# Sliding-window attention: score matmuls in two strips of 64 keys by 320 queries in place of four strips of 32 keys by 288 queries

## The chip, the cores and the metric

The kernel runs on one core of one Trainium2 chip, as a single program. The metric is the device time of one execution in microseconds (us); lower is better. The kernel before took 1099.22 us, the median of three runs (1099.03 to 1101.2). One execution was recorded by the profiler; its rows are quoted below. Engines are named as the profile names them: PE does matmuls, PEld is the load of a matmul's stationary operand (its weights), DVE is the vector engine, ACT the scalar engine, POOL is GpSimd, and SP issues the DMAs.

## What is computed

The reference is one transformer block on 2048 tokens of width 640. Only the attention half is touched by the change:

```python
H = 32; Dh = D // H; W = 256                       # D = 640, so Dh = 20
q, k, v = split(layernorm(x) @ wqkv)               # 32 heads
scores = einsum("bhqd,bhkd->bhqk", q, k) * Dh ** -0.5
mask = (i - j >= 0) & (i - j < W)                  # query i, key j
p = softmax(where(mask, scores, -1e9))
h = x + (p @ v).reshape(B, S, D) @ wo
```

A gated MLP with a spatial 2048 x 2048 projection follows (`h2 = h + B(layernorm(h))`). It comes after the attention in time and is not edited.

## The kernel before, in words

**Stages.** The program first forms V, then Q and K (the lines of `qk_item`, L612 to L614), then runs the attention in one long loop over steps `s`, then the output projection (L118) and the gated MLP. The profile shows the attention loop between 237 and 456 us of the span.

**Units and items.** The 32 heads are taken in 8 groups of 4; the 2048 tokens in 16 blocks of 128. A unit `u` is one group and one block, so there are `NU = 128` units, and each has four items, one for each head `hh`. Queries and keys of a group lie in SBUF tiles (`slot` or `xb`) as rows of bf16 parts: 120 rows for the exact product in three bf16 pieces, and three more rows that carry the row maximum of the softmax.

**The loop.** Step `s` does three things on PE, which are interleaved in an order written by hand (PE, DVE, ACT and SP follow the written order here; POOL's order is set by the planner after step 13):

- `max_item` for unit `s + 18` (L373 matmuls, then a DVE maximum, L383): 128 queries against up to 384 keys, to find each query's largest score. It is written as four strips of 32 queries by 288 keys, each on its own quarter of the array's columns: `tile_position=(0, 32 * j)`. It stops at step 109, when no unit is left.
- `score_item` for unit `s` (L426 matmuls, then the exponential on ACT, L429 or, from step 113, L431 for two heads together): 128 keys against up to 384 queries, with the maximum subtracted by the three extra rows. Only 257 of the 384 queries see a given key, so it too is written as strips, four of 32 keys by 288 queries. After the fourth head, POOL sets what lies outside the window to zero (L433, L436).
- `pv_item` for unit `s - 2` (L454 matmuls, f32): four heads at once, on four tiles of 32 columns, accumulated over the key blocks in a PSUM bank. It is issued in two halves, after heads 1 and 3. Finished banks are copied by ACT (L473) or DVE (L475) and stored.

So with heads 0 to 3 the PE order within a step is max, score, max, score, pv, max, score, max, score, pv. From step 110 the max items are gone. In `max_rows` (L389, once in 8 steps) PE turns the row maxima; DVE, POOL and two DMAs then bring them into the three extra rows, 8 or more steps before they are used.

**Buffers.** The maxima have three PSUM banks, the scores three others; the score of an item waits until the exponential of three items ago has freed its bank. In the last steps three pairs of banks serve two heads each.

**Where a strip crosses token 1024.** The tokens of a group lie in two halves, so `tokens` (L346) splits a strip that crosses the middle into two matmuls.

Of the kernel before, what the change touches and what calls it, by code (L numbers as in the profile page):

```python
# [15 lines left out]
P = 128  # L16
# [18 lines left out]
def block_kernel(ctx, tc, x, xt, wqk, wv, wo, w_in, wsp, bsp, w_out, out):  # L35
    nc = tc.nc
# [225 lines left out]
    with ExitStack() as ab:  # L262
# [54 lines left out]
        def s2_tile():  # L317
            return s_tile(2)
# [27 lines left out]
        def tokens(st, rows, a, hh, t0, n):  # L346

            o = 0
            while o < n:
                c, t = divmod(t0 + o, S // 2)  # L350
                w = min(n - o, S // 2 - t)
                yield o, w, st[c][:rows, a, hh, t:t + w]
                o += w

        def one(st, rows, a, hh, t0, n):
            (_, _, x), = tokens(st, rows, a, hh, t0, n)
            return x
# [47 lines left out]
        def score_item(u, hh):  # L405


            g, kb = divmod(u, NT)
            st = slot_ap[g % 3]
            n = min(384, S - kb * P)  # L410
            if hh == 0:
                p_tiles[u] = tmp3.tile([P, 4, 384], F32, tag="pt", bufs=4, name=f"pt{u}")
            pt = p_tiles[u]
            if u > NU - NT:
                if hh % 2 == 0:
                    bank2.append(bank2.pop(0))
                ps = bank2[-1][:, hh % 2]
            else:
                ps = s2_tile()
            for i in range(4):  # L420
                k0 = kb * P + 32 * i
                b, e = 32 * i, min(n, 32 * i + 288)
                if NU - NT < u and 4 * (u - NU + NT - 1) + hh < 6:
                    b, e = 0, n
                for o, w, q in tokens(st, 123, 0, hh, kb * P + b, e - b):
                    nc.tensor.matmul(ps[32 * i:32 * i + 32, b + o:b + o + w], one(st, 123, 1, hh, k0, 32), q,  # L426
                                     start=True, stop=True, tile_position=(0, 32 * i))
            if u <= NU - NT:
                nc.scalar.activation(pt[:, hh, :n], ps[:, :n], AF.Exp, scale=SCALE)  # L429
            elif hh % 2:  # L430
                nc.scalar.activation(pt[:, hh - 1:hh + 1, :n], bank2[-1][:, :, :n], AF.Exp, scale=SCALE)  # L431
            if hh == 3:
                nc.gpsimd.affine_select(out=pt[:, :, :P], in_=pt[:, :, :P], pattern=[[0, 4], [1, P]], base=0,  # L433
                                        channel_multiplier=-1, compare_op=OP.is_ge, fill=0.0)
                if n == 384:
                    nc.gpsimd.affine_select(out=pt[:, :, 256:], in_=pt[:, :, 256:], pattern=[[0, 4], [-1, P]],  # L436
                                            base=-1, channel_multiplier=1, compare_op=OP.is_ge, fill=0.0)
# [41 lines left out]
        if True:  # L479
# [191 lines left out]
            for n in range(7):  # L671
                w = slice(n % 3 * P, (n % 3 + 1) * P)
# [64 lines left out]
            for n in range(24):  # L737
                q, r = divmod(n, 8)
# [49 lines left out]
        for s in range(NU + 2):  # L788
# [9 lines left out]
            for hh in range(4):  # L798
                if s < 2 and hh == 2:
                    next(dense)  # L800
                if s == 1 and hh == 3:
                    assert next(dense, 0) == 0
                if u1 < NU:
                    max_item(u1 // NT, u1 % NT, hh)
                if s < NU:
                    score_item(s, hh)
                if hh == 1 and u1 % 8 == 0 and s <= NU - LEAD:
                    rows = max_rows((u1 - 8) // NT, (u1 - 8) % NT // 8)
                    next(rows)
                if hh == 3 and u1 % 8 == 1 and s <= NU - LEAD + 1:  # L810
                    next(rows)
                if 2 <= s < NU - 1:
                    if hh == 1:
                        pv = pv_item(s - 2)
                        next(pv, None)
                    if hh == 3:
                        next(pv, None)
                for u in {(NU, 1): [NU - 3], (NU + 1, 0): [NU - 2, NU - 1]}.get((s, hh), []):
                    for _ in pv_item(u):
                        pass  # L820
                if (s, hh) in ((NU, 0), (NU + 1, 3)):
                    if s == NU:
                        psB.close()
                        psW = pool(psB, "psW", space=PSUM)
                    pre_ps.append(proj_o(s - NU, psW.tile([P, 2, 512], F32, tag="wo", bufs=3, name=f"wo_ps{s - NU}")))
# [779 lines left out]
```

## Time and profile before

| | |
|---|---|
| median of three runs | 1099.22 us |
| the profiled execution's own time | 1096.99 us |
| its span | 1095.3 us |
| PE busy | 1073.5 us, 98% |
| ACT busy in the attention loop, 236.9 to 431 us | 179.06 of 194.10 us |
| DVE busy there | 182.65 us |
| PE busy there | 188.11 us |
| score matmuls (L426), mean of one | 273 ns (x1296, the largest group) |
| granted PE clock | 1.00 throughout |

The profile gives each matmul a start and a duration. The durations of neighbouring matmuls overlap, since the array is a pipeline: a matmul with 288 columns is shown as 0.29 us, while the next group starts 0.12 us later. So it is the distance from one start to the next that tells what an operation costs on PE, and a group in a timeline row such as "0.31 ... x4" is four matmuls on four column tiles that start almost together. In a row, `123*32 123x288` means weights of 123 rows by 32 columns, and 288 columns streamed past them.

### The profile page before, as it was taken

The numbers are of one execution on the slowest core, as the hardware profiler recorded it, in microseconds if no ns is written. First come the engines' busy times: TensorE is split into PE (matmuls) and PEld (weight loads), VectorE is DVE, ScalarE is ACT, GpSimd is POOL, SyncE is SP. The second block draws the span as 40 slices with busy tenths as digits, with TensorE's granted clock in tenths as the row PEclk, the third lists the DMA queues.
The fourth block names the chain that finished last, engine by engine and source line by source line (L and its number), as shares of the span: only waits on it lengthen the run. The fifth ranks groups of instructions, "written<-read, shape, count | busy, mean of one in ns | idle before, by whom it ended". The sixth has DMA issues, their size and how long they took to land.

```text
span 1095.3 us, 28703 instructions
## 1 busy us (share of the span) xinstructions
PE 1073.5 (98%) x11045; PEld 967.9 (88%) x11045; DVE 779.6 (71%) x2157; ACT 603.7 (55%) x1257; POOL 308.9 (28%) x446
## 2 busy tenths in 40 slices
PE   8999999999999999999999999999999999999998
PEld 8998886668888787699999998999999899999998
DVE  6643445779999997586677678656556899988674
ACT  4444433249989899766766557433358433333331
POOL 4414445668766677622200012000001000000000
PEclk9999999999999999999999999999999999999999
DMA  7834566465665565679845342242341567684542
GB/s 257 296 117 118 174 212 217 150 214 174 191 186 184 187 192 172 193 217 289 316 179 186 113 135 77 71 142 87 126 150 51 176 230 249 231 280 139 181 156 97
DMA packets 92293, 194.78 MB, mean 178 GB/s; under 512 B 11958, under 2 KB 46278, under 8 KB 88262
## 3 DMA queue, kind: packets, MB, share of 16 engines
q1 hardware_dynamic: 92156, 192.95, 54.0%
q8 instruction: 87, 1.43, 0.5%
q14 instruction: 50, 0.41, 0.1%
HBM read 127.90 MB, written 64.95 MB: 176 GB/s over the span
## 4 chain that ended last, share of the span: by engine, by line
PE 84%; DMA 4%; issue 4%; ACT 3%; DVE 2%; POOL 1%; SPq 1%; ACTq 0%; POOLq 0%; DVEq 0%
PE g L1217 23%; PE zb L1102 8%; PE pv L454 7%; PE bank L373 5%; PE bank L426 5%; PE qk L612 4%; PE qk L613 4%; PE qk L614 4%; PE out_x L1381 3%; PE zx L1042 2%; PE out_v L1381 2%; PE zv L1042 2%; PE zy L1042 1%; PE zw L1042 1%; PE bank L377 1%
## 5 line engine op out<-in xcount | busy, mean ns | idle before, releaser
L429 ACT ACTIVATE pt<-bank 128x384 f32<-128x384 f32 (+1 forms) x452 | 180.5, 486 | 14.5 <-PE bank L426 9.7
L1217 PE MATMUL g<-zl,aw 128*128 128x432 f32 x768 | 168.9, 357 | 1.0 <-ACT zl L864 1.0
L383 DVE CUSTOM_DVE_ANT_0 junk<-bank,strip 128x288 bf16<-128x288 f32 x392 | 155.8, 452 | 9.8 <-PE bank L373 5.6
L864 ACT ACTIVATE aw<-fx 128x512 fp32r<-128x512 f32 (+2 forms) x152 | 86.1, 587 | 128.4 <-DVE fx L858 53.6
L1217 PEld LDWEIGHTS g<-zl,aw 128*128 128x128 f32 x768 | 144.0, 188 | 7.4 <-ACT zl L864 1.4
L858 DVE TENSOR_TENSOR aw<-fx,aw 128x512 fp32r<-128x512 f32 (+2 forms) x152 | 95.7, 638 | 58.8 <-ACT aw L864 53.8
L454 PE MATMUL pv<-pt,v_sb 128*32 128x192 f32 (+3 forms) x1984 | 133.3, 322 | 2.9 <-POOL pt L433 1.2
L1217 PE MATMUL g<-ze,aw 128*128 128x432 f32 x576 | 132.6, 359 | 2.3 <-DVE row L858 2.3
L1217 PEld LDWEIGHTS g<-ze,aw 128*128 128x128 f32 x576 | 107.1, 188 | 9.0 <-DVE row L858 3.7
L433 POOL TENSOR_SCALAR_AFFINE_SELECT pt<-pt 128x512 f32<-128x512 f32 x128 | 82.6, 646 | 58.1 <-ACT pt L429 55.1
L426 PE MATMUL bank<-slot 123*32 123x288 bf16 (+8 forms) x1296 | 94.8, 273 | 1.0 <-ACT pt L429 0.6
L373 PE MATMUL bank<-slot 120*32 120x288 bf16 (+4 forms) x1248 | 91.6, 275 | 3.0 <-issue 2.8
L454 PEld LDWEIGHTS pv<-pt,v_sb 128*32 128x32 f32 x1984 | 64.1, 110 | 10.2 <-POOL pt L433 5.1
L436 POOL TENSOR_SCALAR_AFFINE_SELECT pt<-pt 128x512 f32<-128x512 f32 x112 | 71.0, 634 | 0.0
L426 PEld LDWEIGHTS <-slot 123*32 123x32 bf16 x1728 | 59.3, 96 | 11.5 <-issue 1.7
L858 DVE TENSOR_TENSOR row<-g,row 128x432 f32<-128x432 f32 x80 | 48.3, 603 | 21.3 <-PE g L1217 20.9
L373 PEld LDWEIGHTS <-slot 120*32 120x32 bf16 x1408 | 51.0, 95 | 14.0 <-issue 5.6
L383 DVE CUSTOM_DVE_ANT_0 junk<-bank,mask 128x384 bf16<-128x384 f32 (+2 forms) x120 | 51.4, 444 | 16.6 <-PE bank L377 14.7
L645 POOL TENSOR_TENSOR sg<-rest,sg 128x512 bf16<-128x512 f32 x39 | 45.6, 1169 | 57.7 <-ACT sg L644 45.2
L630 DVE TENSOR_TENSOR rest<-qk,std 128x512 f32<-128x512 f32 x36 | 24.8, 690 | 42.4 <-PE qk L614 41.2
L635 ACT ACTIVATE sg<-rest 128x512 bf16<-128x512 f32 x39 | 24.6, 631 | 54.1 <-DVE rest L630 52.3
L118 PE MATMUL wo_ps<-xb,xb 128*128 128x320 f32 x260 | 52.4, 311 | 0.5 <-DVE mvc L1496 0.5
(289 smaller groups left out, 2534.5 us busy)
## 6 DMA issues: line engine op xcount, KB each, us to landing
slot<-qk_d SPq DMA_DIRECT2D x144, 160.0 KB
fx<-wsp_in SPq DMA_DIRECT2D x32, 512.0 KB
qk_d<-sg SPq DMA_DIRECT2D x39, 384.0 KB
o_d<-ot SPq DMA_DIRECT2D x64, 128.0 KB
xb<-qk_d SPq DMA_DIRECT2D x48, 160.0 KB
fx<-hn_d SPq DMA_DIRECT2D x24, 320.0 KB
z_d<-row SPq DMA_DIRECT2D x16, 432.0 KB
g_d<-row SPq DMA_DIRECT2D x16, 432.0 KB
```

The source lines that it names most:

```text
L373: nc.tensor.matmul(ps[32 * j:32 * j + 32, o:o + w], one(st, 120, 0, hh, q0, 32), k, start=True, stop=True, tile_position=(0, 32 * j))
L383: nc.vector.tensor_tensor_reduce(out=junk[:, :n], in0=ps[:, :n], in1=keep, scale=1.0, scalar=NEG, op0=OP.add, op1=OP.max, accum_out=m_cols ...
L426: nc.tensor.matmul(ps[32 * i:32 * i + 32, b + o:b + o + w], one(st, 123, 1, hh, k0, 32), q, start=True, stop=True, tile_position=(0, 32 * i))
L429: nc.scalar.activation(pt[:, hh, :n], ps[:, :n], AF.Exp, scale=SCALE)
L433: nc.gpsimd.affine_select(out=pt[:, :, :P], in_=pt[:, :, :P], pattern=[[0, 4], [1, P]], base=0, channel_multiplier=-1, compare_op=OP.is_ge ...
L436: nc.gpsimd.affine_select(out=pt[:, :, 256:], in_=pt[:, :, 256:], pattern=[[0, 4], [-1, P]], base=-1, channel_multiplier=1, compare_op=OP. ...
L454: nc.tensor.matmul(ps[32 * hh:32 * hh + 32, a - 512 * c:b - 512 * c], v_sb[:, kb, v0:v0 + 32], pt[:, hh, a - kb * P:b - kb * P], start=fir ...
L858: (eng or nc.vector).tensor_tensor(out=out, in0=a, in1=b, op=op)
L864: nc.scalar.activation(out, a, AF.Copy)
L1042: nc.tensor.matmul(ps, a[x], b[:, y], start=start and m + x + y == 0, stop=stop and m == n - 1 and x == 1, skip_group_check=True)
L1102: nc.tensor.matmul(b[0][:, :HF], a[:, x, kk], win2[0][:, y, kk, h * HF:(h + 1) * HF], start=kk + x + y == 0, stop=kk == KD - 1 and x == 1)
L1217: nc.tensor.matmul(ps, w[m][:, x, k], zc[k][m][:, y], start=start and k + x + y == 0, stop=stop and k == 3 and x == 1, skip_group_check=True)
```

## The change

The score item is made of two strips of 64 keys by 320 queries, each on half of the array's columns, in place of four strips of 32 keys by 288 queries. 320 queries are what the window of 64 consecutive keys needs, rounded up to a multiple of 64. The max items and the pv items keep their tiles of 32 columns. The diff is whole:

```diff
@@ -417,14 +417,14 @@ def score_item(u, hh)
-            for i in range(4):
-                k0 = kb * P + 32 * i
-                b, e = 32 * i, min(n, 32 * i + 288)
+            for i in range(2):
+                k0 = kb * P + 64 * i
+                b, e = 64 * i, min(n, 64 * i + 320)
                 if NU - NT < u and 4 * (u - NU + NT - 1) + hh < 6:
                     b, e = 0, n
                 for o, w, q in tokens(st, 123, 0, hh, kb * P + b, e - b):
-                    nc.tensor.matmul(ps[32 * i:32 * i + 32, b + o:b + o + w], one(st, 123, 1, hh, k0, 32), q,
-                                     start=True, stop=True, tile_position=(0, 32 * i))
+                    nc.tensor.matmul(ps[64 * i:64 * i + 64, b + o:b + o + w], one(st, 123, 1, hh, k0, 64), q,
+                                     start=True, stop=True, tile_position=(0, 64 * i))
```

What it does to PE's order in the middle of the loop is seen at the end of an item. Before, one score item and the pv half behind it stand so (LDWEIGHTS is a weight load; `x4` behind an L454 row stands for the four heads):

```order
L426 LDWEIGHTS slot_0_2008
L426 MATMUL bank_131<-slot_0_2008 32x288
L426 LDWEIGHTS slot_0_2008
L426 MATMUL bank_131<-slot_0_2008 32x288
L426 LDWEIGHTS slot_0_2008
L426 MATMUL bank_131<-slot_0_2008 32x288
L426 LDWEIGHTS slot_0_2008
L426 MATMUL bank_131<-slot_0_2008 32x288
L454 MATMUL pv_1_3639<-pt_3538,v_sb 32x256 x4
L373 LDWEIGHTS xb_98
```

Now a score item stands between the last strips of a max item and the pv half:

```order
L373 MATMUL bank_127<-slot_1_2009 32x288
L373 LDWEIGHTS slot_1_2009
L373 MATMUL bank_127<-slot_1_2009 32x288
L426 LDWEIGHTS slot_1_103
L426 MATMUL bank_132<-slot_1_103 64x320
L426 LDWEIGHTS slot_1_103
L426 MATMUL bank_132<-slot_1_103 64x320
L454 MATMUL pv_3_5647<-pt_5562,v_sb 32x256 x4
L373 LDWEIGHTS xb_97
```

Eight rows have become four, and the first number of their last column has gone from 32 to 64: a score item is now the only work in the loop with 64 columns, and 32-column work stands on either side of it. Over the program PE's list falls from 11238 rows to 8934. In the changed order a change from a 32-column row to a 64-column row comes 440 times up to the last max item, and as often back; of the 440 ways back 228 lead to L373, 196 to L454, 14 to L389 and 2 to L612.

In the last steps, where no max items are left, two score items (two heads) now stand together between pv halves:

```order
L454 MATMUL pv_2_8608<-pt_8613,v_sb 32x192 x4
L426 LDWEIGHTS slot_1_2009
L426 MATMUL pair_8375<-slot_1_2009 64x320
L426 LDWEIGHTS slot_1_2009
L426 MATMUL pair_8375<-slot_1_2009 64x320
L426 LDWEIGHTS slot_1_2009
L426 MATMUL pair_8375<-slot_1_2009 64x320
L426 LDWEIGHTS slot_1_2009
L426 MATMUL pair_8375<-slot_1_2009 64x320
L454 MATMUL pv_2_8608<-pt_8648,v_sb 32x256 x4
```

Eight rows stand here where there were sixteen, and the change between 32 and 64 columns comes 34 times each way, once in two items.

On DVE, ACT and SP nothing moves. On POOL the planner puts the last step of the row maxima (L396) one zeroing later in most groups of eight steps:

```order
L395 CAST m_1_1_3130<-mr_1_3131 32x128
L433 AFFINE_SELECT pt_3116<-pt_3116 128x4x128
L396 TENSOR_TENSOR m_1_1_3130<-mr_1_3131,m_1_1_3130 32x128
L433 AFFINE_SELECT pt_3173<-pt_3173 128x4x128
```

Before, L396 stood directly behind L395.

## Prediction

> **What bounds the kernel now.** The first view to read is the page's busy times and slices: PE is busy nearly everywhere, so the page alone does not say what a faster or slower score item is worth. The second is the busy time by stretch (span, then busy us and instruction count of PE, PEld, DVE, ACT, POOL): the attention loop up to the last max item, and its last steps.
>
> ```profile
> PE 1073.5 (98%) x11045; PEld 967.9 (88%) x11045; DVE 779.6 (71%) x2157; ACT 603.7 (55%) x1257; POOL 308.9 (28%) x446
> 236.90:431.00 194.10, 188.11 (x5666) 159.53 (x5669) 182.65 (x928) 179.06 (x465) 138.06 (x237) 1.00 0.59 185
> 431.00:456.30 25.30, 23.42 (x610) 15.02 (x601) 10.09 (x20) 24.66 (x46) 21.44 (x36) 1.00 0.61 164
> ```
>
> Three engines stand above 92% of the 194.10 us. To tell them apart I read the chain of waits of this stretch by line, and then the timelines of PE, ACT and DVE in its middle.
>
> ```profile
> by line: PE pv L454 34.9%; PE bank L373 28.8%; PE bank L426 27.6%; ACT pt L429 2.9%; issue 2.7%; PE bank L389 1.2%; ACT ot L473 0.9%; PE qk L612 0.4%; PE qk L614 0.4%; PE qk L613 0.2%; DVE junk L383 0.2%; DVE mcol L383 0.0%
> ```
>
> ```profile
> 258.27 0.30 PE L373 MATMUL bank<-slot 120*32 120x288 bf16 x4
> 258.39 0.30 PE L426 MATMUL bank<-slot 123*32 123x288 bf16 x4
> 258.52 0.30 PE L373 MATMUL bank<-slot 120*32 120x288 bf16 x4
> 258.64 0.31 PE L426 MATMUL bank<-slot 123*32 123x288 bf16 x4
> 258.77 0.51 PE L454 MATMUL pv<-pt,v_sb 128*32 128x192 f32 x8
> 259.10 0.31 PE L373 MATMUL bank<-slot 120*32 120x288 bf16 x4
> ...
> 256.39 6.56 ACT L429 ACTIVATE pt<-bank 128x384 f32<-128x384 f32 x16
> ...
> 258.38 0.45 DVE L383 CUSTOM_DVE_ANT_0 junk<-bank,strip 128x288 bf16<-128x288 f32 x1
> 258.76 0.45 DVE L383 CUSTOM_DVE_ANT_0 junk<-bank,strip 128x288 bf16<-128x288 f32 x1
> ```
>
> From start to start, two items take 0.83 us on PE (258.27 to 259.10): four groups at 0.125 and a pv half at 0.33, so 0.415 us for an item. ACT takes 6.56 / 16 = 0.410 us for an exponential, DVE 0.38 us for a maximum. PE is the bound by a hair; the chain agrees, with 2.9% (5.6 us) through ACT's exponentials and 2.7% (5.2 us) "issue", in which PE waited for nothing that is seen. Two things follow. PE time added to an item is paid in full, less at most those 5.6 us. PE time taken away would be worth 0.005 us an item before ACT takes over.
>
> In the last steps, without max items, ACT holds the chain at one step of two double exponentials in 1.38 us (446.38 to 447.76), while PE's own work is two score pairs at 0.25 and 0.65 of pv, 1.15 us:
>
> ```profile
> 446.38 1.02 ACT pt L431 x2
> ...
> 447.76 1.17 ACT pt L431 x2
> ```
>
> ```profile
> 446.42 0.43 PE L426 MATMUL pair<-slot 123*32 123x288 bf16 x8
> 446.67 0.40 PE L454 MATMUL pv<-pt,v_sb 128*32 128x128 f32 x8
> 446.89 0.43 PE L426 MATMUL pair<-slot 123*32 123x288 bf16 x8
> ```
>
> **The change part by part.** *Streaming.* Four strips of 288 columns run at once, one on each quarter of the array: a group costs 0.125 us, not four times that. Two strips of 320 on halves of the array cost 0.125 x 320 / 288 = 0.139 us: +0.014 an item. Half the matmuls and weight loads fall away, but in this stretch they cost no PE time of their own: four matmuls start within 0.01 to 0.02 us (a group lasts 0.30 to 0.31, one of its matmuls 0.288), and the weight loads lie under the group before. So this part gains nothing.
>
> ```profile
> L426 PE MATMUL bank<-slot 123*32 123x288 bf16 x745 | 55.8, 288 | 0.8 <-ACT pt L429 0.5 <-issue 0.3
> ```
>
> *Changing the width of the column tile.* No 64-column tile occurs in this trace. What occurs is the change between 128 columns and tiles of 32, in steps 0 and 1, where the last Q/K products stand between items:
>
> ```profile
> 237.20 0.29 PE L373 MATMUL bank<-slot 120*32 120x288 bf16 x4
> 237.32 0.29 PE L426 MATMUL bank<-slot 123*32 123x288 bf16 x4
> 237.55 0.50 PE L612 MATMUL qk<-xb,w_last 128*128 128x512 f32 x1
> 237.89 0.40 PE L613 MATMUL qk<-xb,w_last 128*128 128x512 f32 x1
> 238.12 0.39 PE L614 MATMUL qk<-xb,w_last 128*128 128x512 f32 x1
> 238.44 0.31 PE L373 MATMUL bank<-slot 120*32 120x288 bf16 x4
> ...
> 237.55 0.19 PEld L612 LDWEIGHTS qk<-xb,w_last 128*128 128x128 f32 x1 [0.24 <-issue]
> 237.66 0.19 PEld L613 LDWEIGHTS qk<-xb,w_last 128*128 128x128 f32 x1
> ...
> 238.44 0.10 PEld L373 LDWEIGHTS <-slot 120*32 120x32 bf16 x4 [0.36 <-issue]
> 238.46 0.10 PEld L426 LDWEIGHTS <-slot 123*32 123x32 bf16 x4
> ```
>
> The group at 237.20 is followed after 0.12 us by one of the same width, the group at 237.32 only after 0.23 by L612: 0.105 us over the 0.125 of a group. The way back is alike: L614 to L373 is 0.32, L613 to L614 0.23: +0.09. The weight loads say why. L613's begins at 237.66, 0.23 before its matmul; those of L612 and L373 begin with their matmuls (237.55, 238.44): across the change of width the load is not pulled ahead. So part of the load is paid too: L612 lasts 0.50 against 0.40 (+0.10, 128 columns of f32), the group at 238.44 lasts 0.31 against 0.29 (+0.015, 32 columns of bf16).
>
> [...]
>
> I take a change between 32 and 64 to cost what one between 128 and 32 does. For each score item: in, 0.105 plus the uncovered load of 64 bf16 columns, taken as 0.025 (by the nearest row, 0.015 for 32 columns of the same type, and not by the 0.10 of f32 weights); out, 0.09 plus 0.015 (32 columns); streaming 0.014. That is 0.249, less 0.005 since two strips start closer together than four: **0.244 us an item**. It is the same whether a max item or a pv half follows, as both have 32 columns.
>
> Bounds from both sides: at least 0.09 + 0.01 in and 0.09 + 0.01 out, 0.20 with nothing for streaming; at most 0.105 + 0.05 in (half of L612's 0.10, for half its columns), 0.105 + 0.025 out, 0.014: 0.30. Below these stands a cost of nothing, since the trace has no row for 32 against 64; it is a rival below, not an end of this sum.
>
> *Sum up to the last max item.* 440 items x 0.244 = 107.4 us. PE then needs 0.66 us an item against 0.41 on ACT and 0.38 on DVE, so the 5.6 us of the chain that went through ACT are covered: 107.4 - 5.6 = +101.8. The 5.2 us of "issue" I leave as they are. Every later instruction of PE, ACT, DVE and POOL in the loop moves back with it; the loads of the next group on SP get more time, not less. The cover works the other way round here: ACT, DVE, POOL (138.06 us) and the DMAs (0.59 of their time) all lie under PE afterwards.
>
> *Sum of the last steps.* Two pairs of items in a step, each with one way in and out: in 0.13, out 0.105, and 4 x 0.014, together 0.52. PE needs 1.15 + 0.52 = 1.67 us against ACT's 1.38, so the stall moves from ACT to PE: +0.29 in each of 15 steps (112 to 126), +4.3.
>
> *POOL.* L396 behind one more zeroing delays the store of the row maxima by about 0.65 us (one L433 of group mean 646 ns), every eight steps, with eight or more steps until the rows are used. Nothing, and if that slack were gone, at most 14 x 0.65 = 9 us.
>
> ```profile
> L433 POOL TENSOR_SCALAR_AFFINE_SELECT pt<-pt 128x512 f32<-128x512 f32 x128 | 82.6, 646 | 58.1 <-ACT pt L429 55.1
> ```
>
> Altogether 101.8 + 4.3 = +106.1 on the profiled execution's 1096.99 us: 1203.1. That execution lies 2.2 us below the median of the runs (1099.22), so I predict **1205 us**. At 0.20 an item, with ACT's and the issue pauses all covered, it is 88 - 10.8 + 15 x (1.15 + 0.40 - 1.38) = +80, 1179; at 0.30, with nothing covered, 132 + 6 = +138, 1237.
>
> **The rivals.**
>
> *No drain between 32 and 64.* A 64-column strip is then just two neighbouring quarters of the array. For it: nothing in the trace shows 32 and 64 to be different kinds of work, and the rows above change to 128 columns, the whole array, which must wait for every quarter anyway. Against it: waiting for the quarters would end with the last streamed column, yet 0.105 us follow it, and the loads are not pulled ahead on the way back either, where all quarters come free at once. It would cost 440 x 0.014 = 6.2 us at most and, if ACT's 5.6 us cover it, about 1: 1100 to 1106, in the middle 1103. [...] No run here shows 32 and 64 side by side.
>
> *Half a drain.* Only the way to the wider tile waits, since only there a load needs columns that several tiles hold. For it: the dearer of the two ways is this one. Against it: L614 to L373 pays 0.09 in the other direction. It gives 440 x (0.13 + 0.014) - 5.6 + 15 x 0.06 = +59 us, 1158.
>
> *Faster.* If 32 and 64 run side by side freely, what is left is half the score instructions: 2304 of PE's 11238 rows. Its place is PE's unexplained pauses in the loop:
>
> ```profile
> PE bank L373 <- issue: 3.4, 5, 1.6
> PE pv L454 <- issue: 1.1, 3, 0.6
> ```
>
> If these come with the number of instructions, about a third of the 5.2 us and some of the split items' starts go, some 4 us: 1095. It decides only where streaming's 6.2 us stay covered by ACT's 5.6, which makes it unlikely: the pauses lie in few places (5 and 3 times), not in proportion to instructions.
>
> That the change might not do what it says is excluded by the order shown ahead: 64x320 stands in PE's list.
>
> **How the numbers follow.** A drain both ways 0.82, because both directions of the only width change in the trace show it; no drain 0.11; half 0.05; faster 0.02. The likeliest case alone reaches from 1179 to 1237. For 8 in 10 I take 1140 to 1240: it holds nearly all of the first case and of the half drain, and leaves out the two small ones. A measurement of this kernel can tell about 0.2% (2.2 us) from no change. Slower by more than that: the drain, the half drain and two thirds of no drain, 0.95; the rest of no drain is the same, 0.03; faster 0.02.
>
> **What would show it.** In the changed profile's PE timeline a score group should start 0.22 to 0.24 us after the max group ahead (now 0.12), and what follows it 0.25 to 0.27 after its start (now 0.125). Its weight loads should begin with its matmuls, not a group earlier. Two items should take 1.3 us, PE's idle and the chain should lie on L426, L373 and L454 with almost nothing on ACT, and ACT's waits for L426 should grow from 9.7 us to about 100:
>
> ```profile
> L429 ACT ACTIVATE pt<-bank 128x384 f32<-128x384 f32 (+1 forms) x452 | 180.5, 486 | 14.5 <-PE bank L426 9.7
> ```
>
> The loop should end near 562 us, in place of 456. If a score group follows a max group after 0.12 us, the drain is wrong and the time lies near 1103; if only one of the two distances has grown, it is the half drain; if both have grown but by another amount, the term of 0.244 is mis-sized, and 440 times the difference is the error.

## The result

The changed kernel took 1194.58 us (median of four runs, 1192.71 to 1196.83) against 1099.12 us for the kernel before (1097.43 to 1101.2): the ratio is 1.0864, with a 95% interval of 1.0844 to 1.0885. It is slower by 95 us, 8.6%.

### The profile after

Where the time went is read from the first and last starts of the lines that bound the stages (minimum, median and maximum duration in ns, then first and last start in us). Before:

```profile
L373 PE MATMUL bank<-slot x1248: 177/286/298, 236.9 to 431.0; 120*32 120x288 bf16 x137, 120*32 120x128 bf16 x13, 120*32 120x256 bf16 x12, 120*32 120x32 bf16 x5
L426 PEld LDWEIGHTS <-slot x1728: 92/97/101, 237.0 to 456.2; 123*32 123x32 bf16 x192
L118 PE MATMUL wo_ps<-xb x220: 305/309/417, 456.6 to 537.8; 128*128 128x320 f32 x110
```

After:

```profile
L373 PE MATMUL bank<-slot x1248: 177/288/297, 237.1 to 525.7; 120*32 120x288 bf16 x137, 120*32 120x256 bf16 x13, 120*32 120x128 bf16 x13, 120*32 120x192 bf16 x4
L426 PEld LDWEIGHTS <-slot x864: 106/106/113, 237.4 to 555.2; 123*64 123x64 bf16 x173
L118 PE MATMUL wo_ps<-xb x220: 305/309/416, 555.4 to 634.0; 128*128 128x320 f32 x110
```

| stretch | before, us | after, us | difference |
|---|---|---|---|
| start to the first max item of the loop | 236.9 | 237.1 | +0.2 |
| loop, to the last max item | 194.1 | 288.6 | +94.5 |
| last steps, to the last score item | 25.2 | 29.5 | +4.3 |
| to the end of the output projection | 81.6 | 78.8 | -2.8 |
| the rest of the span | 557.5 | 556.9 | -0.6 |

The loss lies in the loop. This is PE's timeline in its middle, the answer to the rows at 258 us in the kernel before:

```profile
301.16 0.31 PE L373 MATMUL bank<-xb 120*32 120x288 bf16 x4
301.39 0.33 PE L426 MATMUL bank<-slot 123*64 123x320 bf16 x2
301.65 0.31 PE L373 MATMUL bank<-xb 120*32 120x288 bf16 x4
301.89 0.33 PE L426 MATMUL bank<-slot 123*64 123x320 bf16 x2
302.14 0.64 PE L454 MATMUL pv<-pt,v_sb 128*32 128x256 f32 x8
302.60 0.31 PE L373 MATMUL bank<-xb 120*32 120x288 bf16 x4
```

From a max group to the score group is 0.23 to 0.24 us, from there to what follows 0.25 to 0.26; both were 0.125. The weight loads (PEld) of the same stretch:

```profile
301.39 0.11 PEld L426 LDWEIGHTS <-slot 123*64 123x64 bf16 x2 [0.28 <-issue]
301.65 0.10 PEld L373 LDWEIGHTS <-xb 120*32 120x32 bf16 x4
301.88 0.11 PEld L426 LDWEIGHTS <-slot 123*64 123x64 bf16 x2
302.14 0.16 PEld L454 LDWEIGHTS pv<-pt,v_sb 128*32 128x32 f32 x8
302.38 0.12 PEld L373 LDWEIGHTS <-xb 120*32 120x32 bf16 x4
```

Every load at a change of width begins with its own matmul (301.39, 301.65, 301.88, 302.14). Only the last, behind a pv half of the same width, begins ahead (302.38 for a matmul at 302.60). The chain of waits of the loop by line, and what ACT waited for there (us in all, times, longest):

```profile
by line: PE bank L426 38.1%; PE pv L454 32.4%; PE bank L373 27.7%; PE bank L389 1.2%; PE qk L612 0.3%; PE qk L614 0.2%; PE qk L613 0.2%
ACT pt L429 <- PE bank L426: 78.5, 205, 0.9
```

The chain now runs on PE alone. ACT, which had 2.9% of it, and the "issue" pauses, which had 2.7%, are gone from it, and ACT waits for scores. Over the whole program these waits are 79.5 us, after 9.7 before:

```profile
L429 ACT ACTIVATE pt<-bank 128x384 f32<-128x384 f32 (+1 forms) x452 | 204.8, 471 | 81.5 <-PE bank L426 79.5
```

The prediction had looked for about 100 us here, and for the end of the loop near 562 us, where the last score load stands at 555.2: the signs came as described, with a loop some 7 us shorter.

### The profile page after: what moved, and what is told of

The parts are those of the page before. It is cut to its first block, busy times and chain, and to the rows that moved or that the text cites. A ratio compares the mean times of both kernels' runs of the same rounds, so it can differ in the third digit from the quotient of the medians.

```text
span 1190.9 us, 26400 instructions
## 1 busy us (share of the span) xinstructions
PE 1178.5 (99%) x9893; PEld 940.4 (79%) x9893; DVE 812.5 (68%) x2157; ACT 634.1 (53%) x1257; POOL 310.7 (26%) x446
## 4 chain that ended last, share of the span: by engine, by line
PE 90%; DVE 3%; ACT 2%; DMA 2%; issue 1%; POOL 1%; SPq 0%; POOLq 0%; DVEq 0%; ACTq 0%
PE g L1217 21%; PE bank L426 9%; PE pv L454 9%; PE bank L373 7%; PE wo_ps L118 6%; PE qk L612 4%; PE zb L1102 4%; PE qk L613 4%; PE qk L614 4%; PE out_x L1381 3%; PE zx L1042 2%; PE out_v L1381 2%; PE zv L1042 2%; PE zy L1042 1%; PE zw L1042 1%
## 5 line engine op out<-in xcount | busy, mean ns | idle before, releaser
L429 ACT ACTIVATE pt<-bank 128x384 f32<-128x384 f32 (+1 forms) x452 | 204.8, 471 | 81.5 <-PE bank L426 79.5
L383 DVE CUSTOM_DVE_ANT_0 junk<-bank,strip 128x288 bf16<-128x288 f32 x392 | 179.0, 457 | 65.7 <-PE bank L373 57.5
L454 PE MATMUL pv<-pt,v_sb 128*32 128x192 f32 (+3 forms) x1984 | 131.3, 332 | 0.2 <-POOL pt L436 0.2
L426 PE MATMUL bank<-slot 123*64 123x320 bf16 (+4 forms) x648 | 100.1, 306 | 0.0
L426 PEld LDWEIGHTS <-slot 123*64 123x64 bf16 x864 | 41.3, 107 | 67.9 <-issue 44.0
L373 PE MATMUL bank<-slot 120*32 120x288 bf16 (+3 forms) x1248 | 93.7, 280 | 0.0
L454 PEld LDWEIGHTS pv<-pt,v_sb 128*32 128x32 f32 x1984 | 41.9, 108 | 35.0 <-issue 3.4
L373 PEld LDWEIGHTS <-slot 120*32 120x32 bf16 x1408 | 38.0, 95 | 29.8 <-issue 1.1
```

The source lines that it names most:

```text
L373: nc.tensor.matmul(ps[32 * j:32 * j + 32, o:o + w], one(st, 120, 0, hh, q0, 32), k, start=True, stop=True, tile_position=(0, 32 * j))
L383: nc.vector.tensor_tensor_reduce(out=junk[:, :n], in0=ps[:, :n], in1=keep, scale=1.0, scalar=NEG, op0=OP.add, op1=OP.max, accum_out=m_cols ...
L426: nc.tensor.matmul(ps[64 * i:64 * i + 64, b + o:b + o + w], one(st, 123, 1, hh, k0, 64), q, start=True, stop=True, tile_position=(0, 64 * i))
L454: nc.tensor.matmul(ps[32 * hh:32 * hh + 32, a - 512 * c:b - 512 * c], v_sb[:, kb, v0:v0 + 32], pt[:, hh, a - kb * P:b - kb * P], start=fir ...
```

## The experiments

**The theory**, an assumption when the runs were planned: each change of the column-tile width (32, 64 or 128) in PE's order costs a wait and a weight load that is not pulled ahead, whatever the widths and whichever columns the tiles use. The prediction and the expectations call the wait a drain, and the width a state of the whole array; that the array empties in it is not shown by any trace here. **The main rival**: 64-column work is dear in itself (its weight loads, its streaming, its starts), wherever it stands. Smaller questions were what the longer streaming costs, whether the two widths matter, whether columns that do not overlap escape, and how much of the stretch's waits covers the price.

### Streaming alone

```diff
 for i in range(4):
     k0 = kb * P + 32 * i
-    b, e = 32 * i, min(n, 32 * i + 288)
+    b, e = 32 * i, min(n, 32 * i + 320)
```

> Four strips of 32 keys as before, but 320 queries wide: the longer streaming alone. Theory (the change of column width is what costs): +0.014 us on each of 440 items, 6 us at most, less what ACT's own 0.41 us an item covers; 1099 to 1105 us, about 1102. Rival (the longer strip is a good part of the 95 us): above 1110.

Measured 1101.28 us against 1098.93: ratio 1.0018, interval 0.9998 to 1.0037. Alone, the longer strips cost about 2 us, and the interval holds no change at all. Even if nothing of their 0.014 us an item were covered, they would be 6 of the 95 us.

### One small matmul of 64 columns, and one of 32

To the kernel before, one matmul of 16 queries is added ahead of the four strips, which stay as they are. It is 32 columns wide in the control and 64 in the probe (R below):

```diff
+(_, _, q), = tokens(st, 123, 0, hh, kb * P, 16)
+nc.tensor.matmul(ps[:R, :16], one(st, 123, 1, hh, kb * P, R), q,
+                 start=True, stop=True, tile_position=(0, 0))
 for i in range(4):
```

> The kernel before with one extra matmul of 32 columns by 16 queries ahead of each score item, in a place that the item overwrites. The control for the probe of 64 columns. Theory and rival alike: 16 columns stream in 0.007 us on one quarter of the array, plus some start: 0.01 to 0.03 us an item, 1100 to 1112 us.

> As the probe of 32 columns, but 64 columns wide by 16 queries; the four strips of 32 stay. Theory (each change of width, both ways, drains the array and uncovers the weight load): in 0.105 + 0.025, out 0.09 + 0.015, streaming 0.007, so 0.24 us an item; less the 13 us of waits that were covered in the changed kernel, and 0.7 us in each of the 15 last steps: 1190 to 1208 us. Rival (a 64-column matmul is dear in itself, by its load of 107 ns and its streaming): about 0.1 us an item, 1130 to 1145 us.

Measured: 1105.28 us with 32 columns (ratio 1.0054, 1.0035 to 1.0074), 1195.77 us with 64 (1.0877, 1.084 to 1.0914). The two kernels differ only in whether 16 queries meet 32 keys or 64, 512 times, and by 90 us. PE's timeline of the probe of 64 (L421 is the probe, L429 the strips):

```profile
301.14 0.29 PE L373 MATMUL bank<-xb 120*32 120x288 bf16 x4
301.37 0.20 PE L421 MATMUL bank<-slot 123*64 123x16 bf16 x1
301.50 0.31 PE L429 MATMUL bank<-slot 123*32 123x288 bf16 x4
301.63 0.30 PE L373 MATMUL bank<-xb 120*32 120x288 bf16 x4
```

The probe starts 0.23 us after the group ahead of it in place of 0.125, and the strips start 0.13 us after a probe of 16 columns (0.007 by proportion to the 0.125 of 288, an estimate). The strips and the max group then stand 0.13 apart, as in the kernel before. So the time lies at the two borders and not in the 64-column work. The chain of the loop in this kernel is also free of "issue", although PE has a thousand rows more than before (in the probe of 32, with as many rows, "issue" has 4.4% between 237 and 431 us):

```profile
by line: PE bank L429 35.2%; PE pv L457 23.9%; PE bank L421 19.9%; PE bank L373 19.7%; PE bank L389 0.7%; PE qk L615 0.3%; PE qk L617 0.2%; PE qk L616 0.2%
```

### The same work, half the changes

PE's order becomes max, max, score, score. Once with the strips of 64, once as a control with the strips of 32:

```diff
-if u1 < NU:
+if u1 < NU and hh % 2 == 0:
     max_item(u1 // NT, u1 % NT, hh)
+    max_item(u1 // NT, u1 % NT, hh + 1)
 if s < NU:
     score_item(s, hh)
```

> The changed kernel with PE's order max, max, score, score in place of max, score, max, score: the same work, half the changes of width (220 each way in place of 440 up to the last max item). Theory: two items cost 0.125 + 0.237 + 0.16 + 0.235 and the pv half with 0.02 uncovered, 0.28 us over before in place of 0.49: 220 x 0.28 = 61, less 13 covered, plus 4 in the last steps, less 3 given back later: about 1148 us (1140 to 1156). Rival (64-column work is dear wherever it stands): as the changed kernel, 1190 to 1197 us.

> Control for the order max, max, score, score: the kernel before (all strips of 32) in that order. Theory: no change of width in the loop, PE 0.83 us for two items as before, so 1096 to 1104 us. Rival (the order itself loosens or tightens the waits, so that the 48 us that the order saved in the changed kernel are not the drains alone): outside that.

Measured: 1145.32 us with 64 (ratio 1.0422, 1.038 to 1.0465), 1102.2 us with 32 (1.0029, 1.0009 to 1.0048). The same matmuls in another order cost about half, and the order by itself gives nothing; it costs 2 us. PE's timeline with 64 columns shows one change each way for two items:

```profile
301.21 0.43 PE L373 MATMUL bank<-xb 120*32 120x288 bf16 x8
301.58 0.46 PE L426 MATMUL bank<-slot 123*64 123x320 bf16 x4
301.97 0.43 PE L454 MATMUL pv<-pt,v_sb 128*32 128x128 f32 x8
302.21 0.43 PE L373 MATMUL bank<-xb 120*32 120x288 bf16 x8
```

### More 64-column work, fewer changes

The max items, too, are written in two strips of 64 (queries here) by 320 keys, so that only the pv halves are of another width:

```diff
-skip = 32 if qb > 1 else 0
+skip = 64 if qb > 1 else 0
 if skip:
-    n, keep = 288, strip
-for j in range(4):
-    q0 = qb * P + 32 * j
+    n, keep = 320, strip
+for j in range(2):
+    q0 = qb * P + 64 * j
...
-        nc.tensor.matmul(ps[32 * j:32 * j + 32, o:o + w], one(st, 120, 0, hh, q0, 32), k,
-                         start=True, stop=True, tile_position=(0, 32 * j))
+        nc.tensor.matmul(ps[64 * j:64 * j + 64, o:o + w], one(st, 120, 0, hh, q0, 64), k,
+                         start=True, stop=True, tile_position=(0, 64 * j))
```

> The changed kernel with the max items also in two strips of 64 by 320: twice as much 64-column work, but changes of width only at the pv halves (220 each way). Theory: two items cost 0.164 + 0.139 + 0.139 + 0.235 on the four groups and 0.33 + 0.125 on the pv half, 1.13 us against 1.34 in the changed kernel and 1.11 in its max, max, score, score order: about 1150 us (1142 to 1158). Rival (64-column work is dear in itself): 1195 us or more, since there is more of it.

Measured 1147.17 us, ratio 1.0432 (1.039 to 1.0474). With twice the 64-column groups it is 47 us faster than the changed kernel. The rival is refuted: between groups of 64 the distance is 0.14 us, the streaming of 320 columns, and the loads lie ahead again (those at 301.14 and 301.28 belong to the matmuls at 301.28 and 301.42).

```profile
301.14 0.30 PE L426 MATMUL bank<-slot 123*64 123x320 bf16 x2
301.28 0.30 PE L373 MATMUL bank<-xb 120*64 120x320 bf16 x2
301.42 0.30 PE L426 MATMUL bank<-slot 123*64 123x320 bf16 x2
301.65 0.43 PE L454 MATMUL pv<-pt,v_sb 128*32 128x128 f32 x8
302.01 0.33 PE L373 MATMUL bank<-xb 120*64 120x320 bf16 x2
...
301.14 0.12 PEld L373 LDWEIGHTS <-xb 120*64 120x64 bf16 x2
301.28 0.11 PEld L426 LDWEIGHTS <-slot 123*64 123x64 bf16 x2
```

From there, both pv halves were moved behind the fourth head:

```diff
-if hh == 1:
-    pv = pv_item(s - 2)
-    next(pv, None)
-if hh == 3:
-    next(pv, None)
+if hh == 3:
+    for _ in pv_item(s - 2):
+        pass
```

> As the kernel with the max items in 64-column strips, and both pv halves together after the fourth head: one change of width each way in a step of four items. Theory: a step costs 0.164 + 6 x 0.139 + 0.235 + 0.66 + 0.125 = 2.02 us in place of 2.26: 27 us less over 110 steps, and some 3 less in the last steps: about 1120 us (1112 to 1130). Rival (the price goes with the number of 64-column groups): as the kernel with the pv halves apart.

Measured 1141.79 us, ratio 1.0388 (1.0351 to 1.0425), well above the expected 1112 to 1130. The changes of width halved once more, but only 5 us came back in place of some 30. PE's timeline of one step, and the rows of ACT and DVE with their idle time:

```profile
299.97 0.86 PE L454 MATMUL pv<-pt,v_sb 128*32 128x256 f32 x16
300.76 0.33 PE L373 MATMUL bank<-xb 120*64 120x320 bf16 x2
...
301.34 0.30 PE L373 MATMUL bank<-xb 120*64 120x320 bf16 x2
301.47 0.30 PE L426 MATMUL bank<-slot 123*64 123x320 bf16 x2
301.68 0.33 PE L373 MATMUL bank<-xb 120*64 120x320 bf16 x2
301.89 0.33 PE L426 MATMUL bank<-slot 123*64 123x320 bf16 x2
302.14 0.86 PE L454 MATMUL pv<-pt,v_sb 128*32 128x128 f32 x16
...
301.35 1.64 ACT L429 ACTIVATE pt<-bank 128x384 f32<-128x384 f32 x4 [0.54 <-PE bank L426]
...
301.13 0.49 DVE L383 CUSTOM_DVE_ANT_0 junk<-bank,strip 128x320 bf16<-128x320 f32 x1 [0.44 <-PE bank L373]
```

The two pv halves and the border behind them now take 0.79 us in one piece, in which ACT and DVE run dry (idle 0.54 and 0.44). When the groups come again at 0.14, the three banks fill at once: the fourth max group (301.68) and the fourth score group (301.89) stand 0.21 after what is ahead, in place of 0.14. The step lasts 2.17 us (299.97 to 302.14), not 2.02; over 110 steps this is 16 of the 25 us that did not come, and the rest was not followed up. That these groups wait for a bank is argued from the times: DVE's first maximum is through at 301.62 (301.13 + 0.49) and ACT's first exponential at about 301.76 (301.35 + 1.64 / 4), each 0.06 to 0.13 ahead of the group that needs its bank. The profile itself names no such wait; it calls the pauses of the loads "issue" (35.3 us ahead of L373). Whether more banks would bring the rest was not tried.

### Another pair of widths

Scores on the whole array, in one matmul without strips:

```diff
-for i in range(4):
-    ...
-    nc.tensor.matmul(ps[32 * i:32 * i + 32, b + o:b + o + w], ...)
+for o, w, q in tokens(st, 123, 0, hh, kb * P, n):
+    nc.tensor.matmul(ps[:, o:o + w], one(st, 123, 1, hh, kb * P, P), q, start=True, stop=True)
```

> Scores on the whole array, 128 keys by 384 queries in one matmul; max and pv items keep tiles of 32. Theory (any change of width drains, whatever the two widths): in 0.105 + 0.01, streaming 384 columns 0.16, out 0.09 + 0.015 for each item, 0.255 us over before against 0.244 in the changed kernel: 1192 to 1206 us, about 1199. Rival (the price grows with the difference of the widths, so that 32 to 128 is dearer than 32 to 64): 1220 or more; rival (the whole array is the cheap, untiled case): below 1170.

Measured 1198.21 us, ratio 1.0894 (1.086 to 1.0928). In the starts of PE's rows, a change between 32 and 128 costs what one between 32 and 64 does:

```profile
301.42 0.31 PE L373 MATMUL bank<-xb 120*32 120x288 bf16 x4
301.65 0.34 PE L421 MATMUL bank<-slot 123*128 123x384 bf16 x1
301.92 0.31 PE L373 MATMUL bank<-xb 120*32 120x288 bf16 x4
```

Here it is 0.23 in and 0.27 out, of which 0.16 to 0.17 is the streaming of 384 columns: in the last steps of the kernel before, two groups of 384 columns take 0.33 us, from one start to the next:

```profile
435.54 0.51 PE L426 MATMUL pair<-slot 123*32 123x384 bf16 x8
435.87 0.41 PE L454 MATMUL pv<-pt,v_sb 128*32 128x128 f32 x8
```

### Columns that do not overlap

```diff
-for i in range(4):
-    k0 = kb * P + 32 * i
-    b, e = 32 * i, min(n, 32 * i + 288)
+for r0, r in ((0, 64), (64, 32), (96, 32)):
+    k0 = kb * P + r0
+    b, e = r0, min(n, r0 + r + 256)
```

> Scores in one strip of 64 keys by 320 and two strips of 32 by 288, on columns that do not overlap. Theory (the width of the tile is a state of the whole array, so tiles of two widths never run side by side): an item has the same change in and out as in the changed kernel, and then pays the two strips of 32 on top: 0.237 + 0.257 + 0.125 = 0.62 us for a max and a score item against 0.494; 440 x 0.37 = 163, less 13 covered, plus 18 in the last steps, less 3 given back: about 1264 us (1250 to 1280). Rival (only the columns concerned drain, and tiles of two widths share the array): the strips of 32 run beside the strip of 64, 1195 us or less.

Measured 1252.2 us, ratio 1.1397 (1.1373 to 1.1422), near the low end of what the theory gave. In PE's timeline the first row holds the two strips of 32 of one score item, the second the four strips of the max item behind it:

```profile
301.66 0.30 PE L426 MATMUL bank<-slot 123*32 123x288 bf16 x2
301.66 0.42 PE L373 MATMUL bank<-xb 120*32 120x288 bf16 x4
302.01 0.55 PE L426 MATMUL bank<-slot 123*64 123x320 bf16 x3
302.27 0.51 PE L454 MATMUL pv<-pt,v_sb 128*32 128x128 f32 x8
302.51 0.29 PE L373 MATMUL bank<-xb 120*32 120x288 bf16 x2
```

The strip of 64 runs alone: the row at 302.01 lasts 0.55 for its three strips, where strips that run at once last 0.30 to 0.33, so those of 32 start some 0.25 later, although the timeline shows no other work on their half of the array. Yet the same two strips of 32 start together with the first strips of the next work of 32 columns, L373 at 301.66 and L454 at 302.27. Here tiles of one width overlap on different columns, and tiles of two widths do not. That overlap was not in the estimate of 1264 us.

### How much is covered

Strips of 64 for the first of four heads only:

```diff
-for i in range(4):
-    k0 = kb * P + 32 * i
-    b, e = 32 * i, min(n, 32 * i + 288)
+r = 32 if hh else 64
+for i in range(P // r):
+    k0 = kb * P + r * i
+    b, e = r * i, min(n, r * i + r + 256)
```

> Strips of 64 for the first of the four heads only, strips of 32 for the other three: 110 changes of width each way up to the last max item. Tells how much of the waits in this stretch is covered: 110 x 0.244 = 27 us. As predicted before the change (5.6 us covered): 1120 us. With all the waits of the chain covered (13 us: ACT, issue and the rest): 1113 us. If the bound stays PE but no wait is covered at this smaller load: 1126 us.

Measured 1113.22 us against 1098.7: ratio 1.0126 (1.0106 to 1.0146), that is +12 to +16 us. It agrees with all the waits covered (13 us), and excludes 5.6 (+21). In the chain of this kernel from 237 to 431 us ACT has no part left, and "issue" 1.0%, some 2 us.

## Why the prediction was right

**What bounds the kernel.** PE by a hair over ACT and DVE, so that added PE time is paid: right. Of the 107.4 us that the sum added, 94.5 arrived.

**Streaming, +0.014 an item and at most 6 us; nothing from the halved instructions.** Right in size: 2 us with the four strips of 320, and groups of 320 columns stand 0.14 us apart where the width does not change. That instructions are free here was not tested alone: the probe of 32 columns added 1024 rows to PE and cost 6 us, 0.012 us a probe. The changed kernel has 2304 fewer, and no gain is seen: the distances in its timeline are what the sum gives without one.

**The change of width, both ways, at the price of 128 against 32.** Right, and it was the step that could not be read from the trace of before: that shows no 64 columns, and 0.244 was the author's estimate from its rows of 128 against 32. The prediction gave 0.22 to 0.24 in and 0.25 to 0.27 out; the timeline has 0.23 to 0.24 and 0.25 to 0.26, so a max and a score group take 0.49 us in place of 0.25: +0.24 against the predicted 0.244. That a price taken from the change between 128 and 32 columns fits so closely was not sure beforehand, and the prediction kept 0.18 for other outcomes. The uncovered load of 64 columns, guessed at 0.025, is seen as 0.33 for a group behind a change and 0.30 for one that follows its like (the rows with max items in 64). In the whole-array scores (0.23 in) and the probe of 16 queries (0.23 in, 0.13 out) neither the second width nor the amount of work changed it. What the runs show, for 32 against 64 and for 32 against 128, is the wait, its price of about 0.11 us a border with the load behind it, and the late load; why PE waits is not shown.

**What is covered, 5.6 us: mis-sized.** The prediction let only ACT's 2.9% of the chain disappear and left the 2.7% of "issue" where it was. With PE as the sole bound everything in the chain that was not PE went: 2.9 + 2.7 + 0.9 (ACT's copies) + 0.2 (DVE) = 6.7% of 194 us, 13.0 us. 107.4 - 13.0 = 94.4, and 94.5 was measured; with one head in four it was 27 less 14.5, some 12 us. Two other readings of the missing 13 us are weaker. Short items might pay less: but the two shortest steps of a group of heads took 2.99 us before and 4.88 after (by the starts of ACT's exponentials), 0.236 an item, nearly the full price. And fewer instructions might save time: but with one head in four only a quarter of them fall away, and some 12 us are covered all the same.

**The last steps, +4.3.** Measured +4.3. The steady step goes from 1.38 us, set by ACT, to 1.72, set by PE, where 1.67 was expected; from the first row to the second are eight pairs of heads, four steps:

```profile
537.28 0.46 PE L426 MATMUL pair<-slot 123*64 123x320 bf16 x4
544.16 0.46 PE L426 MATMUL pair<-slot 123*64 123x320 bf16 x4
```

That the sum agrees to a tenth is partly luck. It charged 15 steps with 0.29 each and the ones ahead of them with nothing; but those ahead grew too (from the first two score items behind the last max item to the first two with the full strips again it is 2.65 us before, 431.68 to 434.33, and 3.18 after, 526.72 to 529.90), and a part of the later waits for ACT and POOL stayed.

**POOL's moved instruction, nothing.** Nothing of it is seen: the chain of the loop has no POOL and no DMA.

**What the prediction did not have.** The output projection gave 2.8 us back. Before, PE waited there for DVE:

```profile
PE wo_ps L118 <- DVE mvc L1496: 1.8, 3, 0.8
```

After, this wait of 1.8 us is gone; where the other 1.0 us comes from was not followed up. DVE's first L1496 stands 10.7 us behind the projection's first matmul before (467.3 and 456.6) and 8.7 after (564.1 and 555.4), so DVE is ahead by 2 us; that the slower last steps gave it this lead is argued, not shown. With it the sum is 1097.0 + 0.2 + 94.5 + 4.3 - 2.8 - 0.6 = 1192.6, the profiled execution's 1192.71. The two terms, 7.3 us of cover and 2.8 given back, are the 10 us between the predicted 1205 and the measured 1194.58.

**The rivals.** No drain (1103), half a drain (1158) and faster (1095) all fell with the two distances: both grew. The premise of the last, that PE's unexplained pauses go with the number of instructions, is not settled. The probe of 64 has more instructions and no pause in the chain, but there PE is held up elsewhere, and the pauses may be hidden by that. Where PE is not held up, "issue" has 2.7% of the chain before, 3.7% with the four strips of 320 and 4.4% with the probe of 32, each up to 431 us: it varies with the same number of rows, and it is largest with the most. What these pauses are stays open.

## What to carry to other kernels

Count the changes of column-tile width in PE's order, not only the columns streamed: here each border between widths cost about 0.11 us, the uncovered weight load included, nearly the 0.125 us of a whole group. Keep all tiled work of an interleaved loop at one width, as the kernel before does, or put work of one width together (max, max, score, score halved the loss), and then look at whether the longer stretches starve the engines that read the banks (with both pv halves together ACT and DVE sat idle for 0.54 and 0.44 us). When a change makes one engine the sole bound, ask how much of the chain that is not that engine's work it covers: in this loop it was all 13 us, the unexplained pauses too, and not ACT's 5.6 alone.

## What the runs showed of the hardware

- One matmul of 64 columns by 16 queries among tiles of 32 cost 0.24 us of PE time (0.23 and 0.13 at its borders in place of 0.125; with what was covered, 90 us over 512 of them against a probe of 32), where its streaming alone is estimated at 0.007, by proportion to the 0.125 of 288 columns.
- Tiles of 32 waited for a tile of 64 on columns that the other does not use (0.25 us, strips of 64, 32 and 32), while tiles of 32 from two different items started together (L426 and L373 at 301.66).
- The price was the same from 32 to 64 and from 32 to 128 columns within 0.02 us (0.23 to 0.24 in; out, 0.11 to 0.12 beyond the 0.14 of 320 columns, and 0.10 to 0.11 beyond the 0.16 to 0.17 of 384).
